# Two half-pairs of transposes and one cluster assignment ahead of the first scores, and a third gate/value bank in place of the second transpose bank

## The chip, the cores and the metric

The kernel runs on one core of a Trainium2 chip. The time is device microseconds of one execution; before the change the median of three runs is 350.61 us (349.88 to 351.16). The profiled execution spans 348.5 us, with the TensorE clock granted at 0.999 of full speed on the mean.

TensorE (PE) does matmuls and transposes into PSUM; ScalarE (ACT) and VectorE (DVE) read PSUM; [...] SyncE's queue (SP) issues most transfers. [...] each tile here that matmuls write takes one, except where said.

## The reference, cut to what matters

```python
# attention: q, k, v are (4, 8, 768, 64); 16 centroids for each of the 8 heads
q_assign = argmax(q_n @ c_n^T); k_assign = argmax(k_n @ c_n^T)   # rows and centroids normalised
mask     = q_assign[..., :, None] == k_assign[..., None, :]
scores   = where(mask, (q @ k^T) / sqrt(64), -1e9)
attn_out = softmax(scores) @ v                                   # (4, 8, 768, 64)
# feed-forward over 3072 tokens of 512 features (the 8 heads side by side)
xn  = x / sqrt(mean(x * x) + 1e-6) * rms_g
out = (silu(xn @ w_gate) * (xn @ w_val)) @ w_out                 # w_gate, w_val (512, 1536), w_out (1536, 512)
```

## The kernel before, in words

**Attention.** The 4 x 8 heads are 32 slots, and two heads of a batch are a pair, so there are 16 pairs. A slot's 768 x 768 scores are cut into nine chunks of 512 columns, and a chunk is a *step*: the main loop has 288 of them, slot 0 being steps 0 to 8, slot 1 steps 9 to 17, and so on. The scores stand transposed (keys on partitions). The cluster mask is made part of the score matmul: q and k, in bf16, carry 16 more rows that hold their one-hot assignment (`aug`), and keys of another cluster get a large negative term. After the exponential (`pT`, L308) a slot's probabilities are multiplied with v in the next slot's steps j = 2 to 7 (`pv_group`, L319), and at j = 8 divided by their sums on DVE (`pv_norm`, L329).

**Preparing a pair** has 13 parts, which `prep_parts` returns by name: T0 to T3, four groups of three fp32 transposes of q or k (L201), each into one PSUM tile of `t_tile`, and each copied to SBUF (`qk32`) by DVE (L205) or ACT (L207); CAST to bf16 on POOL (L224); SP, the assignment's matmuls against the centroids (L237); TR, MX, CMP, SCL and BACK on DVE, which turn it into a one-hot matrix (L244 to L265); PLACE, four transfers of that into `aug` (L278); CASTV, the cast of v on POOL (L229). A part follows its producer through the tile's semaphores; a queue runs in its order.

**Feed-forward.** Tokens go in eight halves of 384 (two for each batch), and a half's 1536 hidden columns in 12 blocks. A column *n* (0 to 95) has a gate piece and a value piece, four matmuls each (L407); `n` also carries an output piece (three matmuls, L440) of the half before, so that four columns complete one output tile `dp` of 128 tokens. The gate goes through a tanh on ACT (L412, `th`), then on DVE `uu` (L416) reads the gate's PSUM bank, and `gvT` (L422) reads the value's; these are the last reads of the two banks. `dp` is scaled into `ob` by ACT (L446) in the tail and by DVE (L448) earlier, and sent out. One piece is issued in each step, from step 96 (`FFN0`) on; `pend` and `flush(1)` hold the last read of a piece back until the next piece is issued.

**RMS norm.** For each batch `rms_parts` gives squares with a sum (L350 on ACT, L352 on DVE), the power -1/2 on POOL (L364, L365), the scaling (`norm`, L373, on DVE), and for all but the first half a transposing transfer into `xnT` (L376), which the gate and value matmuls read. Each is bound to a step after the batch's last slot by a `plan`.

**Order.** The order on each engine is written by hand: `at(step, fn)` puts a part at the end of a step's work. After the last scores follows a tail whose steps j count on; column 72, the first of the last batch, begins at j = 24.

**PSUM.** Two banks are held all the time: `ps_pv` ("acc") and `ps_t` ("t"). The other six are `ps_first` (six banks) in the prologue, then two score tiles of three banks (`scw`) up to step 96, called the wide stage here, and from step 96 on two score banks, two gate/value banks, one output bank ("d") and a second transpose bank:

```python
for nm, bufs in (("sc", 2), ("gv", 2), ("d", 1), ("t", 1)):
```

In the tail odd columns take their gate and value tiles from the score banks, and output tiles alternate between "d" and "acc" by the parity of `tl + qh`, where `tl` is the block of 128 tokens in its half. `keep_warm(n)` issues n matmuls on zeros (L129), which only keep TensorE occupied.

Of the kernel before, what the change touches and what calls it, by code (L numbers as in the profile page):

```python
# [8 lines left out]
F32 = mybir.dt.float32  # L9
# [10 lines left out]
def kernel(  # L20
# [12 lines left out]
    nc = tc.nc  # L33
# [3 lines left out]
    P = 128  # L37
# [134 lines left out]
                in_=moe_w_out[j * 3 * P:(j + 1) * 3 * P, :].rearrange("(c p) d -> p c d", p=P))  # L172


    nt = [0]

    def t_tile(name):
        nt[0] += 1
        pool, tag = ps_t, "t"
        if "wide" not in late:  # L180
            pool, tag = ps_first, "f"
        elif "t" in late and nt[0] % 2:
            pool = late["t"]
        return pool.tile([P, HS], F32, name=name, tag=tag)

    def prep_parts(pi):
# [4 lines left out]
        def t_group(g):  # L191
            a, side = divmod(g, 2)
            if qk32[0] is None:
                qk32[0] = prep.tile([P, 4, HS], F32, name="qk32", tag="qk32")
            if pi == 2 and g > 1:
                tp = ((ps_t, ps_pv)[g - 2]).tile([P, HS], F32, name="tp", tag=("t", "acc")[g - 2])
            else:
                tp = t_tile("tp")
            src = loads[pi, side]
            for i in range(TH):  # L200
                nc.tensor.transpose(tp[:, i * P:(i + 1) * P], src[:, a, i * P:(i + 1) * P], ident_f)  # L201
            dst = qk32[0][:, g, :]
            on_dve = (g % 2 == 0 if pi == 0 else g > 1 if pi == 1 else g % 2 if pi == 2 else pi < 7 or g % 2)
            if on_dve:
                nc.vector.tensor_copy(dst, tp)  # L205
            else:
                nc.scalar.copy(dst, tp)  # L207
            state[g] = tp
# [187 lines left out]
    def ffn_piece(n, kind, tail, on_act):  # L396
        half = n // FC
        fc = n % FC
        b, m = divmod(half, 2)
        if kind < 2 and half < 2 * B:  # L400
            if kind == 0 and fc == 0:
                gvT[half] = ffn.tile([P, FC, HS], BF16, name="gvT", tag="gvT")
            w = (wg, wv)[kind]
            pool, tag = (late["sc"], "sc") if tail and n % 2 else (late["gv"], "gv")
            pt = pool.tile([P, CH], F32, name=("gp", "vp")[kind], tag=tag)
            for dc in range(DC):
                nc.tensor.matmul(pt[:, :HS], lhsT=w[:, dc, fc * P:(fc + 1) * P],  # L407
                                 rhs=xnT[b, m][:, :, dc, :],
                                 start=(dc == 0), stop=(dc == DC - 1))
            if kind == 0:  # L410
                th = ffn.tile([P, HS], F32, name="th", tag="th")
                nc.scalar.activation(th, pt[:, :HS], ACT.Tanh, scale=0.5)  # L412
                uu = ffn.tile([P, HS], F32, name="uu", tag="uu")

                def after():
                    nc.vector.scalar_tensor_tensor(uu, th, 1.0, pt[:, :HS], op0=ALU.add, op1=ALU.mult)  # L416
                cur[n] = uu
            else:
                uu = cur.pop(n)

                def after():
                    nc.vector.tensor_tensor(gvT[half][:, fc, :], uu, pt[:, :HS], op=ALU.mult)  # L422
            pend.append(after)
        elif kind == 2 and half >= 1:
            hf = half - 1
            b, m = divmod(hf, 2)
            t = m * TH + fc // 4
            qd = fc % 4
            tl = fc // 4

            nh = 2 if n >= NU + FC - 4 else 1
            qh, nq, N = qd * nh // 4, 4 // nh, DM // nh
            if qd % nq == 0:
                pool, tag = (ps_pv, "acc") if tail and (tl + qh) % 2 else (late["d"], "d")
                cur["d"] = pool.tile([P, DM], F32, name="dp", tag=tag)
            dp = cur["d"][:, 0:N]
            cols = slice(qh * N, (qh + 1) * N)
            for i in range(3 * nh):
                f = (qd % nq) * 3 * nh + i
                nc.tensor.matmul(dp, lhsT=gvT[hf][:, f, tl * P:(tl + 1) * P], rhs=wo[:, f, cols],  # L440
                                 start=(f == 0), stop=(f == FC - 1))
            if qd % nq == nq - 1:
                def after():
                    ob = ffn.tile([P, DM], F32, name="ob", tag="ob", bufs=3)[:, 0:N]
                    if on_act:
                        nc.scalar.activation(ob, dp, ACT.Copy, scale=0.5)  # L446
# [29 lines left out]
    p0, p1, p2 = (prep_parts(pi) for pi in range(3))  # L476
    keep_warm(8)
    for i in (T0, T1, T2, T3):
        p0[i]()
# [12 lines left out]
        p2[i]()  # L492
    p0[PLACE]()
    p0[CASTV]()
    load_part(1, 2, nc.scalar)
    for i in (T1, T3):
        p2[i]()
    p1[CAST]()
    keep_warm(9, w_ps)
    first.close()  # L500
    late["wide"] = wide.enter_context(tc.tile_pool(name="ps_wide", bufs=2, space=PSUM,
                                                 reuse_waits="tile"))
    for i, step in ((SP, 0), (TR, 1), (MX, 1), (CMP, 2), (SCL, 2), (BACK, 3), (PLACE, 3), (CASTV, 3)):
# [10 lines left out]
    for b in range(B):  # L514
# [3 lines left out]
                    (norm, (12, 17, 18), (0, 1, 2)), (turn, (17, 20, 22), (0, 1, 2)),  # L518
                    (sumsq, (27, 29, 30), (3, 4, 5)), (inv, (30,), (1,)), (norm, (32, 33, 34), (3, 4, 5))]
        else:  # L520
            plan = [(sumsq, (9, 9, 10), (0, 1, 2)), (inv, (11,), (0,)), (norm, (12, 13, 15), (0, 1, 2)),
                    (sumsq, (19, 19, 25), (3, 4, 5)), (inv, (26,), (1,)), (norm, (27, 28, 29), (3, 4, 5))]
        for fn, steps, items, *more in plan:
            for step, it in zip(steps, items):
                at(H * NCH * (b + 1) + step, lambda fn=fn, it=it, more=more: fn(it, *more))
    for pi in range(3, B * NP):
        base = 2 * NCH * (pi - 2) + {7: 17, 8: 6}.get(pi, 0)
        steps = (-11, -8, -5, -2, 0, 0, 2, 3, 4, 5, 6, 7, 10)
        if pi == 3:
            steps = (-9, -6, -4, -2, 0, 1, 3, 4, 5, 6, 7, 8, 10)  # L530
        elif pi == 6:
# [69 lines left out]
```

## Time and profile before

| engine | busy us | share of the span |
|---|---|---|
| PE | 335.5 | 96% |
| ACT | 226.1 | 65% |
| DVE | 223.5 | 64% |
| POOL | 89.0 | 26% |

| TensorE waits for | us | times |
|---|---|---|
| `dp` (L440) for ACT's `ob` | 1.9 | 4 |
| `vp` (L407) for DVE's `gvT` | 1.8 | 4 |
| `tp` (L201) for DVE's copy `qk` | 1.5 | 2 |
| `gp` (L407) for the transposing transfer into `xnT` | 0.7 | 1 |

The shares are means over the whole span; the stages differ, and a stage's limit is read from its own stretch. In timeline lines the columns are start and length in us, engine, line, operation, output<-inputs, shapes, count; the bracket names the idle time ahead and what ended it. A matmul's shown length overlaps the next one's: in an unbroken row of matmuls of one kind, starts are 0.22 us apart for 512 columns and 0.16 for 384. The first scores start at 14.32 us, the wide stage ends at about 63.8, the last exponential of the scores starts at 269.93, and column 72 starts at 288.50.

### The profile page before, as it was taken

What the parts mean: (1) busy time and instruction counts of PE and PEld (TensorE: products, weight loads), DVE (VectorE), ACT (ScalarE), POOL (GpSimd) and SP (SyncE); (2) the same over time, 40 slices, a digit from 0 to 9 for tenths busy, and PEclk for the clock granted to TensorE, in tenths of its full rate; (3) what the DMA queues carried; (4) which work ended last, traced back from release to release, by engine and by line L of the source; (5) the groups of instructions that cost most, each with busy time, mean ns of one, the idle gap of its engine ahead of it and who ended that gap; (6) DMA issues with size and microseconds to landing.
All of it is one profiled execution on the core that took longest, in us unless ns stands there. A gap on an engine that the chain in (4) does not pass through costs nothing.

```text
span 348.5 us, 7510 instructions
## 1 busy us (share of the span) xinstructions
PE 335.5 (96%) x2960; PEld 203.5 (58%) x2960; DVE 223.5 (64%) x460; ACT 226.1 (65%) x389; POOL 89.0 (26%) x123
## 2 busy tenths in 40 slices
PE   8988999999999999999999999999999998999996
PEld 4556665666656565565656566656666654555543
DVE  4687698788673777856473678764554686655630
ACT  4688999967867677766767677767777243233322
POOL 2676885086311124230110314100000011000000
PEclk9999999999999999999999999999999999999999
DMA  7666999835944034161501003120000031300012
GB/s 243 226 211 196 229 263 262 213 66 85 247 136 141 30 99 128 41 182 39 170 2 42 32 12 77 40 48 32 30 32 3 30 72 40 74 30 30 32 60 90
DMA packets 36770, 34.98 MB, mean 100 GB/s; under 512 B 13520, under 2 KB 33664, under 8 KB 36736
## 3 DMA queue, kind: packets, MB, share of 16 engines
q1 hardware_dynamic: 30240, 29.20, 26.8%
q0 software_dynamic: 5984, 4.84, 9.2%
q10 hardware_dynamic: 512, 0.48, 0.5%
q8 instruction: 23, 0.38, 0.4%
q14 instruction: 11, 0.09, 0.1%
HBM read 28.61 MB, written 6.29 MB: 100 GB/s over the span
## 4 chain that ended last, share of the span: by engine, by line
PE 80%; DVE 9%; ACT 4%; DMA 3%; issue 2%; POOL 1%; SPq 0%; DVEq 0%; POOLq 0%; ACTq 0%
PE dp L440 17%; PE gp L407 17%; PE vp L407 16%; PE sc L305 11%; PE acc L319 8%; PE tp L201 5%; PE sp L237 3%; PE scw L305 3%; ACT pT L308 2%; DMA aug<-ohT 2%; DVE xn L373 2%; DVE qk L205 1%; DMA xnT<-xn 1%; PE w_ps L129 1%; DVE x L329 1%
## 5 line engine op out<-in xcount | busy, mean ns | idle before, releaser
L308 ACT ACTIVATE pT<-sc 128x512 bf16<-128x512 f32 x192 | 113.5, 598 | 46.9 <-PE sc L305 45.9
L416 DVE SCALAR_TENSOR_TENSOR uu<-th,gp 128x384 f32<-128x384 f32 x96 | 52.9, 551 | 61.2 <-ACT th L412 61.2
L407 PE MATMUL vp<-xnT,wv 128*128 128x384 bf16 x384 | 78.1, 325 | 1.8 <-DVE gvT L422 1.8
L407 PE MATMUL gp<-xnT,wg 128*128 128x384 bf16 x384 | 78.1, 325 | 0.8 <-DMA xnT<-xn 0.7
L440 PE MATMUL dp<-wo,gvT 128*128 128x512 bf16 (+1 forms) x300 | 76.1, 370 | 1.9 <-ACT ob L446 1.9
L412 ACT ACTIVATE th<-gp 128x384 f32<-128x384 f32 x96 | 47.2, 491 | 46.4 <-PE gp L407 43.5
L319 PEld LDWEIGHTS <-pT 128*128 128x128 bf16 x1152 | 57.0, 97 | 28.5 <-issue 2.5
L305 PE MATMUL sc<-aug 80*128 80x512 bf16 (+1 forms) x256 | 72.6, 326 | 0.0
L224 POOL CAST aug<-qk 64x768 bf16<-64x768 f32 x60 | 51.8, 864 | 55.9 <-DVE qk L205 50.0
L319 PE MATMUL acc<-vbf,pT 128*128 128x65 bf16 x1152 | 62.8, 193 | 0.8 <-DVE x L329 0.5
L422 DVE TENSOR_TENSOR gvT<-uu,vp 128x384 bf16<-128x384 f32 x96 | 52.3, 545 | 4.9 <-PE vp L407 0.4
L407 PEld LDWEIGHTS <-wg 128*128 128x128 bf16 x384 | 37.1, 97 | 31.1 <-DMA xnT<-xn 1.2
L308 ACT ACTIVATE pT<-scw 128x1536 bf16<-128x1536 f32 x32 | 44.9, 1457 | 7.3 <-PE scw L305 6.9
L407 PEld LDWEIGHTS <-wv 128*128 128x128 bf16 x384 | 37.0, 97 | 21.0 <-issue 2.7
L440 PEld LDWEIGHTS <-gvT 128*128 128x128 bf16 x300 | 29.1, 97 | 27.0 <-issue 2.9
L305 PEld LDWEIGHTS <-aug 80*128 80x128 bf16 x384 | 33.4, 98 | 18.4 <-issue 7.4
L205 DVE COPY qk<-tp 128x384 f32<-128x384 f32 x40 | 21.9, 553 | 23.5 <-PE tp L201 23.4
L305 PE MATMUL scw<-aug 80*128 80x512 bf16 (+1 forms) x128 | 26.1, 325 | 0.4 <-DMA aug<-ohT 0.2
L364 POOL TENSOR_SCALAR ir<-ss 128x3 f32<-128x3 f32 x7 | 1.6, 235 | 95.7 <-ACT jk L350 84.9
L373 DVE SCALAR_TENSOR_TENSOR xn<-x,ir,g_b 128x512 bf16<-128x512 bf16 x24 | 20.0, 848 | 6.8 <-POOL ir L365 5.8
L229 POOL CAST vbf<-v_in 128x768 bf16<-128x768 f32 x16 | 13.5, 844 | 37.1 <-issue 36.8
L329 DVE TENSOR_TENSOR x<-acc,inv 128x384 bf16<-128x384 f32 x32 | 17.8, 557 | 1.1
(62 smaller groups left out, 212.6 us busy)
## 6 DMA issues: line engine op xcount, KB each, us to landing
q_in<-in_q_dram SPq DMA_DIRECT2D x16, 384.0 KB, 5.5
k_in<-in_k_dram SPq DMA_DIRECT2D x16, 384.0 KB, 6.0
out_dram<-ob SPq DMA_DIRECT2D x23, 256.0 KB, 2.0
v_in<-in_v_dram SPq DMA_DIRECT2D x15, 384.0 KB, 5.5
wg<-in_moe_w_gate_dram POOLq DMA_DIRECT2D x4, 384.0 KB, 8.0
wv<-in_moe_w_val_dram POOLq DMA_DIRECT2D x4, 384.0 KB, 9.4
wo<-in_moe_w_out_dram POOLq DMA_DIRECT2D x4, 384.0 KB, 6.0
aug<-ohT SPq DMA_DIRECT2D x57, 24.0 KB, 1.9
```

The source lines that it names most:

```text
L205: nc.vector.tensor_copy(dst, tp)
L224: nc.gpsimd.tensor_copy(aug[st][a][0:D, :, par * HS:(par + 1) * HS], qk32[0][par * D:(par + 1) * D, 2 * a:2 * a + 2, :])
L305: nc.tensor.matmul(sc[:, o:o + n], lhsT=ag[:, 1, kc * P:(kc + 1) * P], rhs=ag[:, 0, qo:qo + n], start=True, stop=True)
L308: nc.scalar.activation(pts[slot][:, j * CH:(j + nch) * CH], sc[:, :nch * CH], ACT.Exp, scale=scale)
L319: nc.tensor.matmul(acc[:, TORD[g], :], lhsT=pts[slot][:, kc * S + g * P:kc * S + (g + 1) * P], rhs=vb[:, a, TORD[kc], :], start=(kc == 0), ...
L329: nc.vector.tensor_tensor(x_t[b][:, :, h * D:(h + 1) * D], acc[:, :, 0:D], inv.to_broadcast([P, ST, D]), op=ALU.mult)
L373: nc.vector.scalar_tensor_tensor(st["xn"][:, tl, :], x_t[b][:, t, :], st["ir", m][:, tl:tl + 1], g_b, op0=ALU.mult, op1=ALU.mult)
L407: nc.tensor.matmul(pt[:, :HS], lhsT=w[:, dc, fc * P:(fc + 1) * P], rhs=xnT[b, m][:, :, dc, :], start=(dc == 0), stop=(dc == DC - 1))
L412: nc.scalar.activation(th, pt[:, :HS], ACT.Tanh, scale=0.5)
L416: nc.vector.scalar_tensor_tensor(uu, th, 1.0, pt[:, :HS], op0=ALU.add, op1=ALU.mult)
L422: nc.vector.tensor_tensor(gvT[half][:, fc, :], uu, pt[:, :HS], op=ALU.mult)
L440: nc.tensor.matmul(dp, lhsT=gvT[hf][:, f, tl * P:(tl + 1) * P], rhs=wo[:, f, cols], start=(f == 0), stop=(f == FC - 1))
```

## The change

It has five parts.

1. *Prologue.* Pair 3's T0 and T1 and pair 1's SP and TR go ahead of the first scores, among seven fill-in matmuls in place of nine. The load of pair 1's v on ACT's queue goes behind pair 3's two copies, which are on ACT (pair 3's other two stay on DVE). `qk32` gets a third buffer, since pairs 1, 2 and 3 are now held at once. It is for using TensorE's time before the first scores, which the fill-in matmuls take.
2. *Wide stage.* Pair 2's SP moves from step 6 to step 0 and its other parts come some steps earlier; pair 3's remaining parts get a table of their own (T2 at step 4, T3 at 7, SP at 11).
3. *PSUM from step 96 on.* A third gate/value bank replaces the second transpose bank, so `t_tile` gives one bank only. The transposes of pairs 7 to 15 are set two steps apart in place of one, and the bases of pairs 7, 8 and 9 move (from 107, 114 and 126 to 104, 118 and 130).
4. *Last batch's norms.* Squares at tail steps 8, 8, 8 (before 9, 9, 10), power at 9 (11), scaling at 9, 10, 11 (12, 13, 15).
5. *Output tiles in the tail* alternate between the two banks by the parity of `half * 3 + tl + qh`, so that the alternation goes on from one half to the next.

```diff
     def t_tile(name):
-        nt[0] += 1
         pool, tag = ps_t, "t"
         if "wide" not in late:
             pool, tag = ps_first, "f"
-        elif "t" in late and nt[0] % 2:
-            pool = late["t"]
...
-                qk32[0] = prep.tile([P, 4, HS], F32, name="qk32", tag="qk32")
+                qk32[0] = prep.tile([P, 4, HS], F32, name="qk32", tag="qk32", bufs=3)
...
-            on_dve = (g % 2 == 0 if pi == 0 else g > 1 if pi == 1 else g % 2 if pi == 2 else pi < 7 or g % 2)
+            on_dve = (g % 2 == 0 if pi == 0 else g > 1 if pi in (1, 3) else g % 2 if pi == 2 else pi < 7 or g % 2)
...
-                pool, tag = (ps_pv, "acc") if tail and (tl + qh) % 2 else (late["d"], "d")
+                pool, tag = (ps_pv, "acc") if tail and (half * (ST // 2) + tl + qh) % 2 else (late["d"], "d")
...
-    load_part(1, 2, nc.scalar)
     for i in (T1, T3):
         p2[i]()
+    keep_warm(2, w_ps)
+    p3[T0]()
+    p3[T1]()
+    keep_warm(2, w_ps)
+    load_part(1, 2, nc.scalar)
+    p1[SP]()
+    p1[TR]()
     p1[CAST]()
-    keep_warm(9, w_ps)
+    keep_warm(3, w_ps)
...
-    for i, step in ((SP, 0), (TR, 1), (MX, 1), (CMP, 2), (SCL, 2), (BACK, 3), (PLACE, 3), (CASTV, 3)):
+    for i, step in ((MX, 0), (CMP, 1), (SCL, 1), (BACK, 2), (PLACE, 2), (CASTV, 3)):
         at(step, p1[i])
...
-    for i, step in ((CAST, 4), (SP, 6), (TR, 7), (MX, 8), (CMP, 10), (SCL, 11), (BACK, 13), (PLACE, 13), (CASTV, 14)):
+    for i, step in ((CAST, 3), (SP, 0), (TR, 3), (MX, 5), (CMP, 6), (SCL, 8), (BACK, 9), (PLACE, 9), (CASTV, 10)):
         at(step, p2[i])
...
-            plan = [(sumsq, (9, 9, 10), (0, 1, 2)), (inv, (11,), (0,)), (norm, (12, 13, 15), (0, 1, 2)),
+            early = (8, 8, 8, 9, 9, 10, 11) if b == B - 1 else (9, 9, 10, 11, 12, 13, 15)
+            plan = [(sumsq, early[:3], (0, 1, 2)), (inv, early[3:4], (0,)), (norm, early[4:], (0, 1, 2)),
...
-    for pi in range(3, B * NP):
-        base = 2 * NCH * (pi - 2) + {7: 17, 8: 6}.get(pi, 0)
+    for i, step in ((T2, 4), (T3, 7), (SP, 11), (TR, 13), (MX, 14), (CMP, 15), (SCL, 16), (BACK, 18), (PLACE, 18),
+                    (CAST, 18), (CASTV, 28)):
+        at(step, p3[i])
+    at(30, lambda: load_pair(6))
+    for pi in range(4, B * NP):
+        base = 2 * NCH * (pi - 2) + {7: 14, 8: 10, 9: 4}.get(pi, 0)
...
-            steps = (-5, -4, -3, -2, 0, 1, 2, 3, 4, 5, 6, 6, 10)
+            steps = (-8, -6, -4, -2, 0, 0, 2, 3, 4, 5, 6, 6, 10)
...
-            for nm, bufs in (("sc", 2), ("gv", 2), ("d", 1), ("t", 1)):
+            for nm, bufs in (("sc", 2), ("gv", 3), ("d", 1)):
```

More of the change, by code (lines that the diff above doesn't have):

```diff
@@ L172, in w_load @@
                 in_=moe_w_out[j * 3 * P:(j + 1) * 3 * P, :].rearrange("(c p) d -> p c d", p=P))
-    nt = [0]
     def t_tile(name):
-        nt[0] += 1
         pool, tag = ps_t, "t"
@@ L475 @@
     T0, T1, T2, T3, CAST, SP, TR, MX, CMP, SCL, BACK, PLACE, CASTV = range(13)
-    p0, p1, p2 = (prep_parts(pi) for pi in range(3))
+    p0, p1, p2, p3 = (prep_parts(pi) for pi in range(4))
     keep_warm(8)
@@ L525 @@
                 at(H * NCH * (b + 1) + step, lambda fn=fn, it=it, more=more: fn(it, *more))
-    for pi in range(3, B * NP):
-        base = 2 * NCH * (pi - 2) + {7: 17, 8: 6}.get(pi, 0)
+    for i, step in ((T2, 4), (T3, 7), (SP, 11), (TR, 13), (MX, 14), (CMP, 15), (SCL, 16), (BACK, 18), (PLACE, 18),
[4 more added lines that the diff above has]
+        base = 2 * NCH * (pi - 2) + {7: 14, 8: 10, 9: 4}.get(pi, 0)
         steps = (-11, -8, -5, -2, 0, 0, 2, 3, 4, 5, 6, 7, 10)
-        if pi == 3:
-            steps = (-9, -6, -4, -2, 0, 1, 3, 4, 5, 6, 7, 8, 10)
-        elif pi == 6:
+        if pi == 6:
             steps = (-11, -8, -5, -2, 0, 0, 2, 3, 4, 4, 5, 6, 7)
         elif pi > 6:
-            steps = (-5, -4, -3, -2, 0, 1, 2, 3, 4, 5, 6, 6, 10)
+            steps = (-8, -6, -4, -2, 0, 0, 2, 3, 4, 5, 6, 6, 10)
         for fn, step in zip(prep_parts(pi), steps):
```

## The prediction

> **What bounds the kernel now.** I read the busy shares first, then the same shares by stage, then TensorE's waits, then the timeline around each wait.
>
> ```profile
> PE 335.5 (96%) x2960; PEld 203.5 (58%) x2960; DVE 223.5 (64%) x460; ACT 226.1 (65%) x389; POOL 89.0 (26%) x123
> ...
> PE dp L440 <- ACT ob L446: 1.9, 4, 0.7
> PE vp L407 <- DVE gvT L422: 1.8, 4, 0.5
> PE tp L201 <- DVE qk L205: 1.5, 2, 0.7
> ...
> PE gp L407 <- DMA xnT<-xn: 0.7, 1, 0.7
> ```
>
> TensorE (PE) is busy 96% of the span, so work moved about on the other engines is worth nothing by itself: the time can fall only where TensorE waits. The waits columns are total us, number, longest. Three kinds lie in the feed-forward part (`dp`, `vp`, `gp`), one in the first part (`tp`). Shown idle is smaller than the issue time lost, since modelled ends overlap; I take losses from start to start.
>
> ```profile
> 14.30:63.80 49.50, 46.00 (x585) 29.60 (x586) 37.18 (x82) 44.30 (x33) 34.78 (x43) 1.00 0.93 225
> 63.80:270.40 206.60, 204.67 (x1877) 126.47 (x1874) 135.72 (x277) 150.55 (x291) 47.54 (x59) 1.00 0.29 78
> ```
>
> The columns are stretch, length, then busy PE, PEld, DVE, ACT, POOL. In the wide stage (14.3 to 63.8) ACT is busy 44.3 of 49.5, nearly as much as PE: the two pass tiles to each other, and either can be the bound. From 63.8 on PE alone is.
>
> [...]
>
> **Third gate/value bank.** One of the four waits:
>
> ```profile
> 146.58 1.40 DVE L373 SCALAR_TENSOR_TENSOR xn<-x,ir,g_b 128x512 bf16<-128x512 bf16 x2
> ...
> 147.65 0.38 PE L305 MATMUL sc<-aug 80*128 80x256 bf16 x2
> ...
> 147.90 0.54 DVE L422 TENSOR_TENSOR gvT<-uu,vp 128x384 bf16<-128x384 f32 x1
> ...
> 148.50 0.81 PE L407 MATMUL vp<-xnT,wv 128*128 128x384 bf16 x4 [0.46 <-DVE gvT L422]
> ```
>
> The value tile needs the bank of the value tile before it, and `gvT`, which frees that one, stands behind two norms. The two 256-column scores issue in 0.11 each, so `vp` could have started at 147.65 + 0.22 = 147.87; it lost 148.50 − 147.87 = 0.63. The other three, at 77.49, 96.02 and 229.82, lose 0.55, 0.66 and 0.62 in the same way: 2.46 in all. With three banks it needs the bank of the gate tile between, which `uu` freed at 146.11 + 0.54 = 146.65, 1.2 us earlier. Gain 2.46 (range 1.6 to 2.6: DVE, up to 93% busy around 72 to 84, might only pass the lag on).
>
> **One transpose bank instead of two.** From step 96 on each transpose group must find the copy of the one before done. The groups of pairs 7 on are respaced to every 2 steps (every step before); a step there takes 1.1 us at first and 20.2 / 9 = 2.2 us later (a head's nine steps repeat after 20.2 us on the chain), against a copy of 0.48 on ACT or 0.55 on DVE plus one or two operations queued ahead. Hidden: I take 0, bounds 0 and +1.
>
> **Output banks alternate across halves.** In the tail the parity of `tl` alone sent the third block of one half and the first of the next to the same bank. The three like waits and the last:
>
> ```profile
> 313.69 0.59 ACT L446 ACTIVATE ob<-dp 128x512 f32<-128x512 f32 x1
> 314.34 0.81 PE L440 MATMUL dp<-wo,gvT 128*128 128x512 bf16 x3 [0.42 <-ACT ob L446]
> ...
> 336.60 0.60 ACT L446 ACTIVATE ob<-dp 128x512 f32<-128x512 f32 x1 [0.81 <-PE dp L440]
> 337.25 7.96 PE L440 MATMUL dp<-wo,gvT 128*128 128x512 bf16 x48 [0.69 <-ACT ob L446]
> ```
>
> At 281.16, 290.39 and 314.34 the output matmul starts 0.58 later than its four value matmuls of 0.16 allow; at 337.25, with three outputs of 0.22 ahead, 0.85 later. With the new parity blocks go d, acc, d, acc to the end, and no block follows another in its bank by less than four columns. Of 0.58, 0.58, 0.58 and 0.85 the last three are clean gains: 2.01. The first meets the next part.
>
> **Earlier norms of the last batch.** Before, the first half's transpose lands 4.02 after its issue at 284.43, and the gate matmul at 288.50 has lost 0.86 to it. The change moves the squares one step forward and the norms from 12, 13, 15 to 9, 10, 11. Now what queues behind: the first norm waits on DVE for both ACT squares and the power on POOL. The last attention block is scaled at 277.11 + 0.56 = 277.67; two squares at 0.74 spacing and the read of the sum end at 279.17; two POOL operations (0.32 spacing, then 0.88) end at 280.45. Until then DVE stands, with `uu` of column 67 behind the norm. In order at spacings from the trace (norm 0.67, others 0.48): norm 280.48, `uu` to 281.70, norm, `gvT` to 282.83, norm to 283.54. Column 69 wants the banks of column 67 (the score banks, odd columns): without the old `dp` wait its gate matmul could start at 281.23 and must wait for 281.76, and its value matmul, due 282.41, waits for 282.89: two new waits, 1.0. Column 72 then starts at 288.1, not 288.5, and the transpose (issue 283.6, plus 4.0) is in by 287.6. Net gain 0.41 of the 0.58 + 0.86 there. Bounds: −0.3 and 1.44.
>
> **The start.**
>
> ```profile
> 12.03 2.10 PE L129 MATMUL w_ps<-zeros 128*128 128x512 bf16 x9
> 14.32 0.82 PE L305 MATMUL scw<-aug 80*128 80x512 bf16 x4 [0.19 <-DMA aug<-ohT]
> 15.08 0.53 PE L237 MATMUL sp<-qk,cbd 128*32 128x384 f32 x4
> ```
>
> Nine filler matmuls hide the first assignment's transfer. Now two fillers (0.43), pair 3's first two groups (0.33 each), two fillers, pair 1's assignment (0.8), three fillers (0.65). But pair 3's k is issued at 7.18 and lands after 6.7: 13.88. Group two therefore ends at 14.23; then 0.43, 0.85 and 0.65 put the first scores at 16.2, which is 1.9 late, and the first exponential, 0.87 behind, at 17.1.
>
> What comes back: ACT's exponentials can follow each other at 1.34 to 1.43 (of 1.45 each, three take 4.13 and two 2.88), and before, ACT lost 1.40 at 23.64 and 0.88 at 31.82 behind PE, which waited for transposes' copies. Pair 1's assignment and two groups are gone from the first two heads. I follow the new order by hand: exponentials at 17.1, 18.5, 19.9, 21.3; the fifth waits about 0.7, to 23.3, since pair 3's assignment now stands ahead of its scores; the seventh, first of head 2, comes at 26.1 against 25.08. In heads 2 and 3 pair 3's assignment is gone and DVE has done its chain, so ACT runs through: the eleventh at 31.5 against 31.82, the thirteenth at 34.5 against 34.82. From there the order is the old one. So the start costs 1.9 and gets 2.2 back: 0.3 gained, bounds 1.0 gained and 1.9 lost. Pairs 7, 8 and 9 spread out over steps 96 to 130: the same instructions, 0.
>
> **Sum.** 2.46 + 0 + 2.01 + 0.41 + 0.3 = 5.18; 350.61 − 5.18 = 345.4.
>
> **Rivals.**
> 1. The start's delay stays (ACT, 44.3 of 49.5 busy, can't run faster). For: the late exponentials. Against: ACT's own waits of 1.40 and 0.88 are there to fill. 345.4 + 0.3 + 1.9 = 347.6.
> 2. Everything pays: both tail waits go in full (1.0 more) and the start gains 0.3 more. For: `uu` and `gvT` need only be a little earlier than I reckon. 345.4 − 1.3 = 344.1.
> 3. The single transpose bank becomes the wait. Nine pairs have three groups each behind another; at 0.35 each, half of what the wide stage's one bank costs at worst (0.73), 27 × 0.35 = 9.5: 355, slower. For: the wide stage shows two such waits with its one bank. Against: both stand behind a whole assignment chain on DVE; its later pairs, three steps apart, show 0.2.
> 4. The gains are eaten: the start's delay stays (347.6), DVE only passes its lag on and 1.6 of the bank's 2.46 is lost, and the tail falls to its bound of −0.3, 0.7 less: 347.6 + 1.6 + 0.7 = 349.9, no change.
>
> **How the numbers follow.** Forecast 0.54, rival 1 0.17, rival 2 0.16, rival 3 0.06, rival 4 0.07. The range takes rivals 1 and 2 with their margins: 343.8 to 348.1. Faster by over 0.3% (below 349.6): 0.54 + 0.17 + 0.16 = 0.87; the same: 0.06 of rival 4; slower: 0.07, rival 3 and the last 0.01 of rival 4.
>
> **What would show it.** Right: no `vp` wait for `gvT` between 64 and 270; no `dp` wait for `ob`; first scores near 16.2, and the thirteenth exponential within 0.3 of 34.5; around column 69 in the tail gate and value matmuls that wait for `uu` and `gvT`; no wait for `xnT`. Wrong: `tp` waiting for `qk` in the feed-forward part, or score matmuls from 64 on as late as at the start.

## The result, and the profile after

The changed kernel takes 346.39 us (median of four runs, 346.12 to 346.56); the kernel before, run beside it, 350.87 (349.88 to 351.16). The ratio is 0.9877, with a 95% interval of 0.9855 to 0.9898: 4.48 us less, where 5.18 was forecast. The profiled execution spans 344.3 us, before 348.5. In all that follows, lines of the changed kernel and of those built on it are five below the lines of the kernel before (scores L300 for L305, gate and value L402 for L407, output L435 for L440, `uu` L411 for L416, `gvT` L417 for L422, norm L368 for L373).

The busy shares of the changed kernel:

```profile
PE 332.0 (96%) x2925; PEld 202.9 (59%) x2958; DVE 222.2 (65%) x458; ACT 226.9 (66%) x391; POOL 88.9 (26%) x123
```

Nothing in them tells what happened: every share is within a point of what it was. TensorE's waits do (us in total, times, longest):

```profile
PE acc L314 <- DVE x L324: 0.9, 2, 0.6
PE tp L196 <- DMA k_in<-in_k_dram: 0.9, 2, 0.5
...
PE vp L402 <- DVE gvT L417: 0.5, 2, 0.3
PE gp L402 <- DVE uu L411: 0.4, 1, 0.4
```

The waits of `dp` for `ob` (1.9), of `tp` for its copy (1.5) and of `gp` for the transfer (0.7) are gone. None of the four old waits of `vp` for `gvT` is left either: the two shown are new and lie in the tail, as does `gp` for `uu`. New in the start is `tp` for the k transfer, and `acc` for `x`, there too, grew from 0.5 to 0.9. Here are the two stages again, cut where step 96 now starts and where the scores end (length, then busy PE, PEld, DVE, ACT, POOL):

```profile
14.30:64.45 50.15, 47.01 (x587) 29.57 (x586) 35.99 (x80) 44.64 (x34) 34.29 (x42) 1.00 0.92 219
64.45:268.10 203.65, 202.16 (x1853) 126.68 (x1875) 135.58 (x277) 150.56 (x291) 47.37 (x59) 1.00 0.29 80
```

The wide stage has become longer, and the stretch behind it shorter. To split the gain I take the start of the same score matmul in both traces, which no modelled end blurs:

| | before | after | gained since the row above |
|---|---|---|---|
| first score of step 96 starts | 63.76 | 64.43 | −0.67 |
| first score of step 285 starts | 267.41 | 265.08 | 3.00 |
| last matmul starts | 344.94 | 340.56 | 2.05 |
| span ends | 348.5 | 344.3 | −0.2 |

So the start lost 0.67 where 0.3 was to be gained; the middle, which held the third bank, gained 3.00 where 2.46 was forecast; the tail gained 2.05 where 2.01 + 0.41 was. The 0.2 lost behind the last matmul comes with the new start: from that matmul's start to the end of the span it is 3.77 to 3.80 us in the six traces, this one and five below, that have pair 3's first two groups ahead of the first scores, and 3.55 to 3.57 in the other eight. What it is stays open.

**The tail.** The timeline of the changed kernel around column 69, with the idle time ahead in the bracket:

```profile
278.23 0.75 DVE L368 SCALAR_TENSOR_TENSOR xn<-x,ir,g_b 128x512 bf16<-128x512 bf16 x1 [1.69 <-POOL ir L360]
278.89 0.55 DVE L411 SCALAR_TENSOR_TENSOR uu<-th,gp 128x384 f32<-128x384 f32 x1
279.36 0.75 DVE L368 SCALAR_TENSOR_TENSOR xn<-x,ir,g_b 128x512 bf16<-128x512 bf16 x1
279.50 0.81 PE L402 MATMUL gp<-xnT,wg 128*128 128x384 bf16 x4 [0.44 <-DVE uu L411]
280.02 0.55 DVE L417 TENSOR_TENSOR gvT<-uu,vp 128x384 bf16<-128x384 f32 x1
280.62 0.81 PE L402 MATMUL vp<-xnT,wv 128*128 128x384 bf16 x4 [0.32 <-DVE gvT L417]
```

This is the forecast's picture: VectorE stands idle for 1.69 until the power on GpSimd (POOL) is there, the norm goes first because it is first in the queue, and `uu` and then `gvT` come behind. From start to start the two matmul groups lose 0.61 and 0.48, together 1.09 (forecast 1.0). A third wait was not forecast: at 292.63, in column 75, the value tile waits for a `gvT` that stands behind two norms of the second half, 0.33 lost. The old losses of 0.58, 0.58, 0.58, 0.85 and 0.86 are all gone: 3.45 − 1.09 − 0.33 = 2.03, which is the tail's 2.05.

**The start.** The timeline of the changed kernel, in two parts:

```profile
14.11 0.52 PE L196 MATMUL tp<-ident_f,k_in 128*128 128x128 f32 x3 [0.51 <-DMA k_in<-in_k_dram]
...
16.65 0.81 PE L300 MATMUL scw<-aug 80*128 80x512 bf16 x4
...
24.36 1.13 DVE L249 TENSOR_TENSOR oh<-tr,mx 128x384 bf16<-128x384 f32 x1
25.52 0.73 DVE L255 TENSOR_SCALAR oh<-oh 64x384 bf16<-64x384 bf16 x1
26.39 0.56 DVE L324 TENSOR_TENSOR x<-acc,inv 128x384 bf16<-128x384 f32 x1
27.00 0.36 PE L314 MATMUL acc<-vbf,pT 128*128 128x65 bf16 x6 [0.60 <-DVE x L324]
```

Pair 3's k lets its transposes go at 14.11 (forecast 13.88), and the first scores start at 16.65 (16.2). Later, slot 0's division `x`, which frees the accumulator that slot 1 needs, stands on VectorE behind pair 3's compare and scale; from start to start TensorE loses 0.77 to it at 27.00. ScalarE's exponentials in the same trace, a line for each unbroken row of them:

```profile
17.50 5.68 ACT L303 ACTIVATE pT<-scw 128x1536 bf16<-128x1536 f32 x4 [2.35 <-DMA v_in<-in_v_dram]
23.88 8.30 ACT L303 ACTIVATE pT<-scw 128x1536 bf16<-128x1536 f32 x6 [0.70 <-PE scw L300]
32.43 4.45 ACT L303 ACTIVATE pT<-scw 128x1536 bf16<-128x1536 f32 x3 [0.24 <-PE scw L300]
```

The 0.70 ahead of the fifth is as forecast. The first is 0.4 late against the forecast (17.50 for 17.1) and the seventh still 0.46 (26.56 for 26.1); the eleventh is 0.93 late (32.43 for 31.5) and the thirteenth 0.92 (35.42 for 34.5). So 0.4 was lost before the first scores, and another 0.5 in head 2, where `x` is waited for. The thirteenth is 0.60 behind the kernel before (34.82), and step 96 is 0.67 behind it: what the start lost by then is never given back.

### The profile page after: what moved, and what is told of

It reads as the page before. It is cut to its first block, busy times and chain, and to the rows that moved or that the text cites. A ratio compares the mean times of both kernels' runs of the same rounds, so it can differ in the third digit from the quotient of the medians.

```text
span 344.3 us, 7504 instructions
## 1 busy us (share of the span) xinstructions
PE 332.0 (96%) x2925; PEld 202.9 (59%) x2958; DVE 222.2 (65%) x458; ACT 226.9 (66%) x391; POOL 88.9 (26%) x123
## 4 chain that ended last, share of the span: by engine, by line
PE 84%; DVE 7%; ACT 3%; DMA 3%; issue 2%; POOL 1%; POOLq 0%; DVEq 0%; SPq 0%; ACTq 0%
PE gp L402 17%; PE vp L402 17%; PE dp L435 16%; PE sc L300 12%; PE acc L314 9%; PE tp L196 5%; PE sp L232 3%; PE scw L300 2%; DMA k_in<-in_k_dram 2%; ACT pT L303 2%; PE w_ps L129 1%; DVE qk L200 1%; DVE oh L249 1%; DVE x L324 1%; DVE xn L368 1%
## 5 line engine op out<-in xcount | busy, mean ns | idle before, releaser
L411 DVE SCALAR_TENSOR_TENSOR uu<-th,gp 128x384 f32<-128x384 f32 x96 | 53.0, 552 | 66.5 <-ACT th L407 66.3
L402 PE MATMUL gp<-xnT,wg 128*128 128x384 bf16 x384 | 78.1, 325 | 0.6 <-DVE uu L411 0.4
L402 PE MATMUL vp<-xnT,wv 128*128 128x384 bf16 x384 | 78.2, 326 | 0.5 <-DVE gvT L417 0.5
L407 ACT ACTIVATE th<-gp 128x384 f32<-128x384 f32 x96 | 47.2, 492 | 43.6 <-PE gp L402 41.0
L300 PE MATMUL sc<-aug 80*128 80x512 bf16 (+1 forms) x256 | 73.0, 327 | 0.0
L435 PE MATMUL dp<-wo,gvT 128*128 128x512 bf16 (+1 forms) x268 | 71.3, 369 | 1.6
L417 DVE TENSOR_TENSOR gvT<-uu,vp 128x384 bf16<-128x384 f32 x96 | 52.6, 548 | 5.9 <-PE vp L402 0.8
L402 PEld LDWEIGHTS <-wg 128*128 128x128 bf16 x384 | 37.2, 97 | 30.7 <-issue 1.3
L402 PEld LDWEIGHTS <-wv 128*128 128x128 bf16 x384 | 37.1, 97 | 19.1 <-issue 0.9
L435 PEld LDWEIGHTS <-gvT 128*128 128x128 bf16 x300 | 29.1, 97 | 24.4
L300 PEld LDWEIGHTS <-aug 80*128 80x128 bf16 x384 | 33.1, 98 | 17.2 <-issue 7.1
L200 DVE COPY qk<-tp 128x384 f32<-128x384 f32 x38 | 20.7, 553 | 17.0 <-PE tp L196 16.9
L300 PE MATMUL scw<-aug 80*128 80x512 bf16 (+1 forms) x128 | 26.1, 326 | 0.4 <-issue 0.4
L368 DVE SCALAR_TENSOR_TENSOR xn<-x,ir,g_b 128x512 bf16<-128x512 bf16 x24 | 20.4, 862 | 6.8 <-POOL ir L360 5.7
L202 ACT COPY qk<-tp 128x384 f32<-128x384 f32 x26 | 12.3, 479 | 11.0 <-PE tp L196 10.8
```

Source lines behind the costliest of these rows:

```text
L300: nc.tensor.matmul(sc[:, o:o + n], lhsT=ag[:, 1, kc * P:(kc + 1) * P], rhs=ag[:, 0, qo:qo + n], start=True, stop=True)
L368: nc.vector.scalar_tensor_tensor(st["xn"][:, tl, :], x_t[b][:, t, :], st["ir", m][:, tl:tl + 1], g_b, op0=ALU.mult, op1=ALU.mult)
```

## The experiments

All were timed in five rounds beside the kernel before, whose median was 350.67 to 350.82 in these sets. "Gained" is against that median.

**The bank with its spacing, alone.** On the kernel before:

```diff
-        elif "t" in late and nt[0] % 2:
-            pool = late["t"]
-        base = 2 * NCH * (pi - 2) + {7: 17, 8: 6}.get(pi, 0)
+        base = 2 * NCH * (pi - 2) + {7: 14, 8: 10, 9: 4}.get(pi, 0)
-            steps = (-5, -4, -3, -2, 0, 1, 2, 3, 4, 5, 6, 6, 10)
+            steps = (-8, -6, -4, -2, 0, 0, 2, 3, 4, 5, 6, 6, 10)
-            for nm, bufs in (("sc", 2), ("gv", 2), ("d", 1), ("t", 1)):
+            for nm, bufs in (("sc", 2), ("gv", 3), ("d", 1)):
```

> The kernel before with only the third gate/value bank, the single transpose bank and the two-step spacing of pairs 7 to 15 (the part after step 96). My theory: the four value matmuls' waits for gvT go, 2.46 us by the prediction, 3.0 by the traces of before and after (step 96 to step 285): 347.9 to 348.4 us against 350.9, and a trace with no value matmul waiting for gvT between 64 and 270 us. Rival (the gain of that stretch came from the prologue and the wide stage, which hand a shorter queue on): no more than 1 us gained.

Measured: 347.60 us, ratio 0.991 (0.9897 to 0.9923), 3.07 gained; and its trace shows no TensorE wait at all between 64 and 270. From step 96 to step 285 it takes 200.65 us, as the changed kernel does, against 203.65 before: the bank and the spacing together are the whole 3.00 of the middle.

**The bank, with the old spacing.** The same without the lines of `base` and `steps`.

> As the run with the bank and the steps, but the old spacing and bases of the transposes of pairs 7 to 15 (one step apart) on the single transpose bank. Theory: the bank alone gives 2.46; where the groups stand one step apart the next must wait for the copy of the one before, 9 pairs x 3 groups, so part of it is lost: 0.3 us per group in the first pairs, where a step takes 1.1 us, and near 0 later, where it takes 2.2 us: 348.0 to 350. Rival 3 of the prediction (the single bank as the wait): 27 x 0.35 = 9.5 us lost, near 358. If the spacing does nothing, the same time as the run with it.

Measured: 349.85 us, ratio 0.9976 (0.9969 to 0.9984), 0.82 gained. The old spacing, with the old bases, takes 3.07 − 0.82 = 2.25 of the bank's gain away. The traced execution is the slowest of the sixteen (350.81), but its excess lies in the start, where it waited 1.3 for a k transfer; from step 96 to 285 it takes 202.82, which is 2.17 more than with the spacing. Its timeline shows two of the new waits:

```profile
79.43 0.55 PE L196 MATMUL tp<-ident_f,q_in 128*128 128x128 f32 x3 [0.36 <-DVE tr L239]
...
80.61 0.55 PE L196 MATMUL tp<-ident_f,k_in 128*128 128x128 f32 x3 [0.22 <-ACT qk L202]
```

Transposes wait for the copy that empties their one bank, or for what is queued ahead of it. Four such waits, all of pairs 7 to 9, lose 0.41, 0.53, 0.39 and 0.39 from start to start, 1.72 of the 2.25; the rest is not accounted for. Later pairs, whose steps are twice as long, show none.

**The output banks' parity, alone.** On the kernel before:

```diff
-                pool, tag = (ps_pv, "acc") if tail and (tl + qh) % 2 else (late["d"], "d")
+                pool, tag = (ps_pv, "acc") if tail and (half * (ST // 2) + tl + qh) % 2 else (late["d"], "d")
```

> The kernel before with only the parity of the output tiles in the tail changed. Theory: the waits at 290.39, 314.34 and 337.25 go, 2.01 us, and the one at 281.16 only turns into a longer wait for the last batch's transposed rows: 348.9 us, with a gate matmul of column 72 that loses 1.4 us in place of 0.86. Rival (all four are gains): 348.3. Rival (the tail is held by ACT or DVE anyway): under 0.7 us gained.

Measured: 349.08 us, ratio 0.9953 (0.9941 to 0.9965), 1.59 gained. All four waits for `ob` are gone. TensorE's waits from 270 on in its trace:

```profile
PE gp L407 <- DMA xnT<-xn: 1.3, 1, 1.3
PE vp L407 <- DVE gvT L422: 0.2, 1, 0.2
```

From start to start the first loses 1.46, where before it lost 0.86: the first of the four losses was only passed on to the transfer, as forecast. The second, at 295.47 in column 75, loses 0.32 and is new. 2.59 − 0.60 − 0.32 = 1.67: the forecast's 2.01 lacked the last term.

**The changed kernel with the old norm steps.**

```diff
-            early = (8, 8, 8, 9, 9, 10, 11) if b == B - 1 else (9, 9, 10, 11, 12, 13, 15)
+            early = (9, 9, 10, 11, 12, 13, 15) if b == B - 1 else (9, 9, 10, 11, 12, 13, 15)
```

> The changed kernel with the last batch's squares, power and norms back at tail steps 9, 9, 10, 11, 12, 13, 15. Theory: the two waits of column 69 for uu and gvT (0.61 + 0.48 lost in the changed kernel) go, and column 72's gate matmul waits 1.46 for the transposed rows instead, as in the run with the parity alone: 346.39 + 1.46 - 1.09 = 346.8 us. So moving the norms is worth 0.4, as forecast, and not 1.44. Rival (the norms' move is worth the whole of 1.46): 347.8.

Measured: 346.46 us, ratio 0.9875 (0.9861 to 0.989), 0.07 above the changed kernel, which is nothing. In its trace, from 270 on:

```profile
PE gp L402 <- DMA xnT<-xn: 0.9, 1, 0.9
```

From start to start that is 1.09, and the move replaces it by 0.61 + 0.48 = 1.09. The stretch from one and the same late score matmul to the end of the span says it again: 344.3 − 267.18 = 77.12 in the changed kernel, 345.2 − 268.05 = 77.15 here. (The traced execution is the slowest of its four, by a stretch at half clock in the start, 20.40 to 23.80, which this leaves out; see the last section.) Moving the norms traded a wait for a transfer for two waits on VectorE's queue.

**The norms behind the columns.** If those two waits come from the norms' place in the queue, the early transfer can be had without them: squares as in the change, norms later and closer.

```diff
-            early = (8, 8, 8, 9, 9, 10, 11) if b == B - 1 else (9, 9, 10, 11, 12, 13, 15)
+            early = (8, 8, 8, 9, 11, 12, 12) if b == B - 1 else (9, 9, 10, 11, 12, 13, 15)
```

> The changed kernel with the squares as early as it has them (8, 8, 8) and the power at 9, but the three norms at tail steps 11, 12, 12, so that uu and gvT of column 67 stand ahead of them on VectorE. Theory (a queue that runs in order lets uu and gvT wait behind the first norm, which waits for the power): both waits of column 69 go and the transposed rows still land before column 72 asks for them: 346.39 - 1.09 = 345.3 us. Rival (the norms would then be too late for column 72): 346 to 346.8.

Measured: 345.16 us, ratio 0.984 (0.9827 to 0.9853), 1.23 below the changed kernel. Each taken against the kernel before beside it, it is 1.05, and so it is from the late score matmul to the end: 343.2 − 267.13 = 76.07 for 77.12. From 270 on only this is left, column 75's wait:

```profile
PE vp L402 <- DVE gvT L417: 0.2, 1, 0.2
```

Same squares, same power, same norms, and neither the columns nor the transfer wait. That shows the cause: a norm that waits for GpSimd holds up all that stands behind it on VectorE.

**The changed kernel with the old start.** Prologue, tables and loop of pairs 1 to 3 as before, the rest as changed; the core of it:

```diff
-    keep_warm(2, w_ps)
-    p3[T0]()
-    p3[T1]()
-    keep_warm(2, w_ps)
-    load_part(1, 2, nc.scalar)
-    p1[SP]()
-    p1[TR]()
-    keep_warm(3, w_ps)
+    keep_warm(9, w_ps)
```

> The changed kernel with the prologue and the wide stage of before (pairs 1 to 3 as before; the bank, the spacing, the parity and the earlier norms of the last batch kept). Theory: the new start costs 0.67 us by the traces (step 96 at 64.43 against 63.76), so this one is faster than the changed kernel by that: 345.7 us, step 96 at 63.8. Rival (the new start pays, later, by what it takes from DVE and TensorE in the first steps after 96): 347 us or more.

Measured: 345.72 us, ratio 0.9867 (0.9848 to 0.9887), 0.67 below the changed kernel; each taken against the kernel before beside it, 0.47. The two intervals overlap, so the times alone would not settle it. The traces do: step 96 at 63.97 here and 64.43 in the changed kernel, 0.46 apart, and another 0.2 behind the last matmul. In the other traces with the old start it stands at 63.73 to 63.85, but for the bank with the old spacing, whose trace waited for a late k (64.77); in the other two with the new start unaltered at 64.37 and, with 3.4 us at half clock, at 65.29. The new start costs time, 0.4 to 0.7 by step 96.

**Pair 3's compare and scale behind the division.** Is it the wait for `x`, or the late first scores?

```diff
-    for i, step in ((T2, 4), (T3, 7), (SP, 11), (TR, 13), (MX, 14), (CMP, 15), (SCL, 16), (BACK, 18), (PLACE, 18),
+    for i, step in ((T2, 4), (T3, 7), (SP, 11), (TR, 13), (MX, 14), (CMP, 17), (SCL, 18), (BACK, 19), (PLACE, 19),
```

> The changed kernel with the compare, scale, back-transpose and place of pair 3 at steps 17, 18, 19, 19 instead of 15, 16, 18, 18, so that the division of slot 0 (x) stands ahead of the compare on VectorE. Theory A (of the 1.0 us between forecast and trace at the start, about 0.5 is this wait: at 27.00 the next slot's accumulation lost 0.77 to x, which stood behind pair 3's chain): that wait goes and step 96 comes 0.4 to 0.6 earlier, 345.9 us. Theory B (only the late first scores count, and ScalarE runs at its rate behind them): no change, 346.4.

Measured: 346.36 us, ratio 0.9876 (0.9861 to 0.9891), the changed kernel's time. The loss at `x` fell from 0.77 to 0.31, yet step 96 starts at 64.19, only 0.24 earlier. And in this execution the first scores started at 15.42, 1.2 earlier than in the changed kernel's trace, without a gain that matches: pair 3's third group of transposes starts at 18.98 here and at 19.16 there, since it waits for VectorE to read pair 2's assignment, and the third scores stand behind it. Why that was not earlier either, its timeline shows (start, length):

```profile
14.04 3.70 POOL L219 CAST aug<-qk 64x768 bf16<-64x768 f32 x4
...
15.91 1.17 DVE L249 TENSOR_TENSOR oh<-tr,mx 128x384 bf16<-128x384 f32 x1
17.12 0.73 DVE L255 TENSOR_SCALAR oh<-oh 64x384 bf16<-64x384 bf16 x1
```

The same compare took 0.60 and the same scale 0.25 in the changed kernel's trace, at 17.14 and 17.77, where no cast ran beside them: 1.05 more. The expectation of 345.9 by the wait for `x` alone fell. It is a part: from the seventh exponential to the thirteenth it is 8.53 us here and 8.86 in the changed kernel.

**Pair 1's cast behind its assignment.** To take GpSimd's cast off VectorE's early chain, on the changed kernel:

```diff
-    p1[CAST]()
-    for i, step in ((MX, 0), (CMP, 1), (SCL, 1), (BACK, 2), (PLACE, 2), (CASTV, 3)):
+    for i, step in ((MX, 0), (CMP, 1), (SCL, 1), (BACK, 2), (PLACE, 2), (CAST, 2), (CASTV, 3)):
```

> The changed kernel with pair 1's cast on GpSimd moved behind its place (from the prologue to step 2), so that no GpSimd cast runs while VectorE makes pair 1's one-hot. Theory ([...] 1.17 and 0.73 us where they overlap the cast, 0.60 and 0.25 where they don't): both short in every profile, and the third group starts up to 1 us earlier where pair 3's k lands early; the time falls by 0 to 0.5, 345.9 to 346.4. Rival (the two lengths have another reason): the compare still over 0.9 in a profile in which the assignment of pair 1 starts before 14.5.

Measured: 345.93 us (345.04 to 346.53), ratio 0.9859 (0.9846 to 0.9873); the interval overlaps the changed kernel's, so no gain in time is shown. The trace does show what slowed the compare:

```profile
16.07 0.59 DVE L249 TENSOR_TENSOR oh<-tr,mx 128x384 bf16<-128x384 f32 x1
16.70 0.25 DVE L255 TENSOR_SCALAR oh<-oh 64x384 bf16<-64x384 bf16 x1
```

With the cast at 19.36, both are short though early, pair 3's third group of transposes starts at 18.09, and step 96 at 63.33. That is 1.1 earlier than in the changed kernel's trace, but not by the cast alone: the first scores start at 15.59 here, and the traced execution is the fastest of its four. Against the run before, with its first scores at 15.42, step 96 is 0.86 earlier.

**Pair 3's transposes not ahead of the scores.** If the late first scores are the cost, take what delays them out of the prologue. VectorE then makes all four of pair 3's copies:

```diff
-            on_dve = (g % 2 == 0 if pi == 0 else g > 1 if pi in (1, 3) else g % 2 if pi == 2 else pi < 7 or g % 2)
+            on_dve = (g % 2 == 0 if pi == 0 else g > 1 if pi == 1 else g % 2 if pi == 2 else pi < 7 or g % 2)
-    keep_warm(2, w_ps)
-    p3[T0]()
-    p3[T1]()
-    keep_warm(2, w_ps)
+    keep_warm(3, w_ps)
-    for i, step in ((T2, 4), (T3, 7), (SP, 11), (TR, 13), (MX, 14), (CMP, 15), (SCL, 16), (BACK, 18), (PLACE, 18),
+    for i, step in ((T0, 4), (T1, 7), (T2, 9), (T3, 11), (SP, 12), (TR, 13), (MX, 14), (CMP, 15), (SCL, 16), (BACK, 18), (PLACE, 18),
```

> The changed kernel with pair 3's first two groups back behind the first scores (steps 4 and 7, its others at 9 and 11, its assignment at 12, all copied by VectorE), and six fill-in matmuls; pair 1's assignment stays ahead of the first scores. Theory: the first scores are no longer held by pair 3's k, which lands at 13.9, so they start at 14.4 to 14.6 and step 96 comes about 0.7 to 1.2 earlier than in the changed kernel: 345.2 to 345.7 us. Rival (TensorE's load in the first two slots is what counts, and the two groups are better done early): 346.4 or more.

Measured: 349.29 us (347.95 to 351.42), ratio 0.9953 (0.9938 to 0.9968): almost 4 us above what was expected, though the first scores started at 14.36 as intended. Its stretches behind the first two groups of scores (the figure behind the bracketed counts is the granted clock):

```profile
16.00:19.20 3.20, 1.91 (x11) 0.86 (x9) 2.49 (x6) 2.11 (x2) 3.01 (x5) 0.99 0.06 15
19.20:29.40 10.20, 9.88 (x67) 6.00 (x67) 5.82 (x12) 5.04 (x4) 7.53 (x10) 0.50 0.65 209
```

and the same stretches of the changed kernel:

```profile
16.00:19.20 3.20, 2.99 (x20) 0.99 (x18) 2.97 (x6) 1.61 (x2) 1.09 (x2) 1.00 0.34 117
```

TensorE ran at half its clock for 10.2 us, after a stretch in which it was busy only 1.91 of 3.20. The expectation reckoned with the same clock. That is a part of the miss and not the whole: each of the sixteen executions has its mean granted clock, and the one that kept it whole (0.999) took 347.95, over 2 us more than was expected; the other fifteen have 0.984 to 0.995 (by estimate from the trace with the old norm steps, where the clock is 0.50 for 3.4 us, such a stretch in 346 us takes 0.005 off the mean) and took 348.28 to 351.42.

**The same with fill-in matmuls in that gap.** Five matmuls on zeros more, into a bank that is free then:

```diff
+    at(3, lambda: keep_warm(5, ps_pv.tile([P, CH], F32, name="w2", tag="acc")))
```

> The run with pair 3's groups behind the first scores (349.3 us, TensorE's clock granted at one half from 19.2 to 29.4 us), with five more fill-in matmuls on zeros, on the still unused accumulator bank, in step 3, in front of the transposes that wait there for VectorE. They take 1.1 us in a wait of 1.3, and give nothing to the result. Theory [...]: the clock stays whole, the exponentials keep ScalarE's rate, and the time falls to 345.5 to 346.5 us. Rival (the clock has nothing to do with that wait, or the order of the parts itself costs the 3 us): 349 or more.

Measured: 347.62 us (346.64 to 348.95), ratio 0.9914 (0.9894 to 0.9934), 1.67 below the run without them, and in the traced execution (347.07) the clock stays whole:

```profile
16.00:19.20 3.20, 3.20 (x24) 1.54 (x16) 2.26 (x5) 2.80 (x2) 3.08 (x5) 1.00 0.23 82
19.20:29.40 10.20, 7.68 (x93) 4.76 (x92) 7.50 (x15) 7.18 (x6) 9.45 (x12) 1.00 0.66 211
```

Of the six executions three kept the clock (0.999 or more; 346.64 to 347.07), and three did not (0.994 to 0.995; 348.16 to 348.95). So filling the gap helped, with three of six whole against one of sixteen, but it did not settle the clock. And with a whole clock the time is still above the 345.5 to 346.5 that were expected: step 96 starts at 65.59, and the largest new loss is 1.70 at 28.21, where `acc` waits for `x` behind the crowded assignment chains. Behind the scores at these steps pair 3's transposes cost more than ahead of them. The old start has them behind the scores as well, but at steps 9, 12, 14 and 16, with pair 2's assignment first, and that costs less.

**Only its last two groups and its assignment later.**

```diff
-    for i, step in ((T2, 4), (T3, 7), (SP, 11), (TR, 13), (MX, 14), (CMP, 15), (SCL, 16), (BACK, 18), (PLACE, 18),
+    for i, step in ((T2, 7), (T3, 9), (SP, 12), (TR, 13), (MX, 14), (CMP, 15), (SCL, 16), (BACK, 18), (PLACE, 18),
```

> The changed kernel with pair 3's third and fourth group at steps 7 and 9 and its assignment at 12 (from 4, 7 and 11), so that each stands behind the scores that it now holds up. Theory (the start costs 0.67 because TensorE, in order, stands at the third group until pair 2's transposed assignment has been read, at 19.1 us however early the first scores were, and the fifth exponential waits 0.7 to 0.8 behind pair 3's assignment): the third and fifth exponentials no longer wait, step 96 comes 0.5 to 1.0 earlier: 345.4 to 345.9 us. Rival (the late first scores alone count): no change, 346.4.

Measured: 347.42 us, but six times from 345.22 to 348.76; ratio 0.9908 (0.9884 to 0.9931). The traced execution is the fastest of them, with a whole clock and step 96 at 63.52, 0.9 earlier than in the changed kernel's. The granted clocks part the six: three kept it (0.999 or more) and took 345.22, 345.98 and 346.63; three have 0.993 to 0.995 and took 348.22 to 348.76. So where the clock holds, this order is about as fast as was expected (345.4 to 345.9); but half of the executions lose about 2 us with the clock, and the median is above the changed kernel's.

**The parts that pay, put together.** The old start, the third bank with its spacing, the parity, the norms behind the columns, and the second half's norms two steps apart against column 75's wait. What differs from the run with the old start:

```diff
-            early = (8, 8, 8, 9, 9, 10, 11) if b == B - 1 else (9, 9, 10, 11, 12, 13, 15)
+            early = (8, 8, 8, 9, 11, 12, 12) if b == B - 1 else (9, 9, 10, 11, 12, 13, 15)
-                    (sumsq, (19, 19, 25), (3, 4, 5)), (inv, (26,), (1,)), (norm, (27, 28, 29), (3, 4, 5))]
+                    (sumsq, (19, 19, 25), (3, 4, 5)), (inv, (26,), (1,)), (norm, (27, 29, 31) if b == B - 1 else (27, 28, 29), (3, 4, 5))]
```

> The changed kernel with the prologue and wide stage of before, the last batch's first norms at tail steps 11, 12, 12, and its second three at 27, 29, 31 (from 27, 28, 29), so that uu and gvT of a column stand ahead of them. If the parts add up: 346.39 - 0.67 (start) - 1.09 (column 69's two waits) - 0.33 (column 75's wait) = 344.3 us, and no gate or value matmul of the tail waits for VectorE. Rival (the start's gain and the tail's overlap, or other waits come up): 345 or more.

Measured: 344.82 us (344.04 to 345.20), ratio 0.9818 (0.9786 to 0.985), the lowest median of all (the interval overlaps that of the norms behind the columns); span 342.3. That is 0.5 above the 344.3 that the parts add up to. Between 64 and the end TensorE waits for nothing that the profile shows. What is left is the old start's own:

```profile
PE tp L196 <- DVE qk L200: 1.5, 2, 0.7
...
PE tp L196 <- DVE tr L239: 0.5, 1, 0.5
```

## Why the prediction was right, and where it failed

The total was right within 1.0 us: 346.39 for 345.4, inside the range, and faster. Part of that is luck, since the terms miss both ways: the middle gained 0.54 more than was forecast, the tail 0.37 less, and the start 0.97 less. Term by term:

- **Third gate/value bank**, 2.46: right in mechanism, too small. No value matmul waits for `gvT` between 64 and 270. The middle gained 3.00 in the change and 3.07 alone, 0.5 to 0.6 more than the four waits. It came early: of the 3.00, steps 96 to 144 gained 1.60, and the two waits in there only 0.55 + 0.66 = 1.21. The remaining 0.4 is my reading, not shown: the spread of pairs 7, 8 and 9, which was costed at 0, also removes small delays between the old, denser transposes.
- **One transpose bank**, 0: right with the spacing given. The rival that saw a wait there was right about the mechanism, but only for the old spacing, and wrong about its size: it costs 2.25 there, not 9.5. So the spacing is no ornament of the change; it is what lets the bank be given up.
- **Output banks**, 2.01: right that three losses are clean gains and the first only meets the transfer (0.86 became 1.46). Too large alone (1.59), by the new wait of 0.32 in column 75: with the old wait gone, columns come sooner to a `gvT` behind two norms. I had followed this for column 69 and not for column 75.
- **Earlier norms**, 0.41: the two waits were forecast at 1.0 and measured 1.09, and no transfer is waited for. What they replace was mis-sized: I took 0.58 + 0.86 = 1.44, and with the rest of the change in place it is 1.09. Net 0.07 in time. (In the kernel with the parity alone the transfer's wait was 1.46, as I took. The difference is the transfer itself: from its issue to the matmul that waits for it are 4.10 us there, 288.64 − 284.54, and 3.72 with the old norm steps, 286.69 − 282.97. Why it was shorter is open.)
- **The start**, 0.3 gained: this step failed. 0.67 was lost by step 96 in the traces of before and after, and undoing it gained 0.46 there. The mechanism, first scores late and then idle time of ScalarE filled, was there: late by 2.25 (16.65 for 14.40 with the old start), mostly won back. Two terms were missed. The first stands ahead of the third exponential. In the changed kernel's trace the k transfer was 0.23 later than reckoned and the work behind it took 0.2 more, which carries to the first exponential (0.4). But an earlier k would not have helped: in the four traces that have this start up to there, the third exponential starts at 20.22 to 20.39 (forecast 19.9), though the first scores start anywhere from 15.42 to 16.65, since TensorE, in order, stands at pair 3's third group until VectorE has read pair 2's assignment. And "In heads 2 and 3 pair 3's assignment is gone and DVE has done its chain, so ACT runs through" was wrong: VectorE was still in pair 3's chain when slot 0's division came due, TensorE lost 0.77 to that, and the eleventh exponential another 0.5. I had followed TensorE and ScalarE by hand, and VectorE's queue only at pair 3's assignment.

Two things within VectorE's chain were in no step. The compare took 1.17 beside the cast (15.91 in the run with pair 3's compare and scale behind the division) and 0.60 without it (17.14 in the changed kernel's trace), the scale 0.73 and 0.25. For the compare the traces show more, that it goes by which of the two starts first. In the first 60 us of the traces of before and after there are 14 of these compares. Nine meet no cast and take 0.58 to 0.60. Four start inside a running cast, and each of them ends 0.44 to 0.45 us after that end. One, in the trace of before, starts just ahead of a cast and keeps its 0.59, and then the cast is the longer one, 1.09 where most casts of v take 0.82 to 0.84:

```profile
20.54 0.59 DVE L254 TENSOR_TENSOR oh<-tr,mx 128x384 bf16<-128x384 f32 x1
20.69 1.09 POOL L229 CAST vbf<-v_in 128x768 bf16<-128x768 f32 x1
```

The slow compare at 24.36 in the changed kernel's trace is one of the four: a cast runs from 24.22 to 25.04, and the compare ends at 25.49. Where pair 3's compare and scale stand between two casts, in the run with its transposes not ahead of the scores (27.90 and 28.52), they take 0.59 and 0.25. So the casts cost 0.53 + 0.48 = 1.01 us right ahead of the division that TensorE waits 0.77 for. That the wait would be gone without them is an estimate from these lengths; no run tried it.

The "thirteenth exponential within 0.3 of 34.5" was the test that told the failure: it came at 35.42.

What stays open is how the 0.67 splits. The wait for `x` is one part, since less of it gave an earlier step 96 (64.19); the pacing of pair 3's third group by VectorE's chain another, which bounds what an earlier first score can bring.

## What to carry to other kernels

When a bank is moved from one rotation to another, look at the spacing of the work that loses it: here the third bank was worth 3.07 us with the transposes two steps apart (and three bases moved) and 0.82 without. A wait on a slow producer at the head of an in-order queue is paid by all that stands behind it, so put the waiting instruction where its operand is ready: the same three norms cost 1.09 at steps 9, 10, 11 and nothing at 11, 12, 12. And when work is moved ahead of a start-up, follow every in-order queue, not only the two engines that bound the stage.

## What was not expected of the hardware

TensorE's granted clock was 0.50 for 10.2 us (19.20 to 29.40) in the run with pair 3's transposes not ahead of the scores, and for 3.4 us (20.40 to 23.80) in the run with the old norm steps, which has the changed kernel's own start. In the stretches shown before and behind these it was 0.99 to 1.00. Ahead of them TensorE was busy 1.91 of 3.20 us (16.00 to 19.20) in the one trace, and 4.79 of 6.10 (14.30 to 20.40) in the other. The longest TensorE waits shown there are 1.29 (until 18.01) and 1.25 (until 19.13).

Whether a lack of work takes the clock away these runs do not tell. In the same place the run with pair 3's compare and scale behind the division waited 1.21 (until 18.98) and kept the clock, with a mean of 1.000. With the parity alone TensorE waited 1.30 for the tail's transfer (until 288.64) and was busy, by the lengths in its timeline, about 1.9 of 3.20 us (286.75 to 289.95), and the clock was kept too, with a mean of 1.000. So neither the longest wait nor the busy share, as the profile counts them, decides alone.

It matters for the time as much as the reordering does: in the run with pair 3's last two groups later the executions that kept the clock have a median of 345.98, the others of 348.22. The changed kernel kept it in all four of its executions (1.000), but the run with the old norm steps, which has the same start, lost it in one of four (0.994).
